# Checks and their sums placed otherwise in the score part, z on a third PSUM bank, one L tile given for a fifth row buffer

## The chip, the cores and the metric

The kernel runs on one core of a Trainium2 chip. Its engines are TensorE (PE, matrix products), VectorE (DVE), ScalarE (ACT), GpSimd (POOL) and SyncE (SP, which mostly issues transfers). Each takes its own list of instructions strictly in order, and they wait for one another by semaphores. What is measured is the device time of one execution in microseconds (us); smaller is better.

## The reference

2048 rows of 512 numbers are normalised, and three things are added up for each: the row itself, a Fourier mixing (FNet), and a layer of 4096 tiny experts, of which each of 32 heads picks two by a product of two key sets.

```python
x = A_x;  xn = layernorm(x)                       # (1, 2048, 512)
# FNet: real part of the transform along both axes
a = einsum("bsd,ed->bse", xn, dft_hid_re);  b = einsum("bsd,ed->bse", xn, dft_hid_im)
fnet = einsum("ts,bse->bte", dft_seq_re, a) - einsum("ts,bse->bte", dft_seq_im, b)
# product-key experts: 32 heads, two scores of 64 keys each, K = 2
q = einsum("nd,dhc->nhc", xn, w_q);  q1, q2 = q[..., :128], q[..., 128:]
s1 = einsum("nhd,ed->nhe", q1, k1);  s2 = einsum("nhd,ed->nhe", q2, k2)
i1, i2 = top2(s1), top2(s2);  t1, t2 = the scores there
cand = t1[..., :, None] + t2[..., None, :];  top_s, top_e = top2 of the four
g = softmax(top_s)                                # weights of 2 experts per head
act = gelu(einsum("nd,nhkd->nhk", xn, u[top_e]))  # u, v: (4096, 512)
out = x + fnet + einsum("nhk,nhk,nhkd->nd", g, act, v[top_e])
```

## The kernel before

**Layout.** The 2048 rows are 16 row blocks of 128. Three parts follow one another. The Fourier part takes the first 75 us and is not touched. The **score part** (about 75 to 470 us) runs 8 rounds `j`, four heads each, over 16 row blocks `i`; step `16*j + i` is the number `n` by which the tables of the code place work. The **expert part** (about 470 to 1137 us) computes the layer for 14 of the 16 blocks with dense products over all 4096 experts, and for the last two blocks row by row from gathered expert rows (`NS = 2`).

**One step of the score part.** `scores` runs 12 matmuls into a PSUM tile `s` (L796; four banks in turn), ACT copies it to the tile `ss` (L801), and DVE takes the maxima and their places from `ss` (L804, L808). A bank of `s` is free for PE again only when ACT has copied it. Beside this the engines prepare later work, each piece hung behind a given step: pieces of u and v split into two halves (`fill_uv`: ACT L606 and L607, then POOL L608), the next query weights (ACT L161, POOL L169), `m_stage` (PE L147, ACT L222), and `routing` of the round before, on POOL and DVE (L645 to L689).

**Checks.** The kernel tests symmetries of the Fourier matrices, since it uses only part of them. 32 checks are "early": `check_load` loads a tile `cx` (pool of 3 buffers) three steps ahead; at step `n` its differences are taken on POOL (`cx[k][0]`: L752, L758, and for some L760, L773); later ACT adds up their absolute values (`cx[k][1]`: L778, 896 numbers a partition). `hold` hangs a piece behind a given matmul in the order of DVE, ACT and POOL. The table `at_k` gives the steps.

**One block b of the expert part.** `u_part` computes z for 8 groups of columns `cg`, 48 matmuls of 128 columns each (L956), into a PSUM bank; ACT turns each bank into `act` (L959). `g_mm` builds for each of 4 groups of 32 tokens one-hot tiles on DVE: two tiles `L` (L980), taken in turn from the list `LS`, and one `R` (L988, L991) from `RS`; 32 matmuls turn them into g (L993). `w_part` multiplies act by g on DVE (`w`, L1004), ACT casts it (L1011), DVE takes the rest (L1014). `v_part` is 96 matmuls into one bank `pv` (L1023), and `finish` adds it to y on DVE (L1038). PE's order in one block is z groups 0 to 2, g group 0, z 3 to 6, g 1, z 7, 36 matmuls of v of the block before, g 2, 48 of v, g 3, the last 12 of v, and the next block.

**PSUM banks there.** `pb` has two banks, `pc` two, `pg` four (two tiles g of two banks). z takes the banks of `pb` in turn. One bank of `pc` holds `px`, the row block in use by the gathered rows, for as long as its 64 rows last; the other is `pv`.

**Gathered rows.** 128 rows (2 blocks of 64 pairs of head and pick) pass, spread evenly over the blocks, through `fetch` (POOL L1049: an indirect transfer of 128 rows of u and v together into a tile `ga` of 4 KB a partition, `BUFS` tiles in turn), `dot` (DVE L1065), `gain` (ACT L1075 to L1078, POOL L1083 adds to the output), after which the next fetch is issued. DVE also runs the later checks and ACT their sums.

Of the kernel before, what the change touches and what calls it, by code (L numbers as in the profile page):

```python
# [10 lines left out]
F16 = mybir.dt.float16  # L11
# [8 lines left out]
P = 128  # L20
# [16 lines left out]
def tile_fnet_peer(ctx, tc, x, ca, cb, c5, wt, wf, wr, wq, kt, ut, vn, uv, out):  # L37
# [518 lines left out]
    def part_b(safe, stS, stP, stE, xt, u_sb, cmp_p):  # L556
# [55 lines left out]
        z = sp.tile([P, NT, 3, 2, 2, H], F16, name="z")  # L612
# [90 lines left out]
        def follow(i, after):  # L703
            tc.add_manual_dep(i, after.ins.name, mybir.DependencyInfo(
                mybir.DependencyClass.NoSync, mybir.DependencyReason.DATA), reason="pace")

        def hold(f, after, engines=(mybir.EngineType.DVE, mybir.EngineType.Activation, mybir.EngineType.Pool)):
            made = nc.cur_bb.bb.instructions
            first = len(made)
            f()  # L710
            for i in made[first:]:
                if i.engine in engines:
                    follow(i, after)
                if i.engine == mybir.EngineType.Activation and after.ins.name in GL:
                    follow(i, GL[after.ins.name])
# [109 lines left out]
        else:  # L825
# [7 lines left out]
            for j in range(1, NCH):  # L833
                for t in range(4):
                    todo[1 + t if j == 1 else (j - 1) * NT + 2 * t - 5].append(
                        lambda at, j=j, t=t: m_prep(j, t, wqp, sw))
# [10 lines left out]
        checks = {}  # L847
        cx = {}

        def check_load(k):  # L850
            cx[k] = compare(EARLY[k], k)

        at_k = [10, *(16 + i for i in (0, 4, 6, 7, 10)), *(16 * j + i for j in range(2, 7) for i in (0, 4, 6, 7)), 112, 125]
        assert len(at_k) == len(EARLY)
        for k, n in enumerate(at_k):
            checks.setdefault(n - 3, []).append(lambda mm, k=k: check_load(k))
            checks.setdefault(n, []).append(lambda mm, k=k: hold(cx[k][0], mm))
            checks.setdefault(n + 1, []).append(lambda mm, k=k: hold(cx[k][1], mm))
        XB = {}
        m_stage(1, wq_tile, 0)  # L860
        pend = None
        for j in range(NCH):
# [8 lines left out]
            for i in range(NT):  # L871
                spare, mm = scores(j, i, vals, idx)
# [37 lines left out]

        ap0 = stE.enter_context(tc.tile_pool(name="ap0", bufs=1, side="left"))
        lr = stE.enter_context(tc.tile_pool(name="lr", bufs=1, side="left"))
        LS = [lr.tile([P, 16, P], F16, name=f"L{k}") for k in range(3)]
        RS = [lr.tile([P, 32, NC], F16, name=f"R{k}") for k in range(2)]
        ap = [ap0, stE.enter_context(tc.tile_pool(name="ap1", bufs=1, side="left"))]

        def blk_tiles(b):
            if b == 1:
                xb = bp.tile([P, 2, 2, KD, P], F16, tag="ga", name="xb_1", bufs=BUFS)[:, 0]
            elif b:  # L920
                xb = xbp.tile([P, 2, KD, P], F16, tag="xb", name=f"xb_{b}", bufs=1)
            else:
                xb = XB[0]
            act = ap[b % 2].tile([P, NC, P], F32, tag="act", name=f"act{b}")
            return xb, act
# [2 lines left out]
        alloc_v(V2, 16)  # L928
        TG = 32
        WB = 4  # L930
        BUFS = 4
        BT = [blk_tiles(b) for b in range(2)]
        NB = NT if safe else NT - NS
        ACT = {}
# [11 lines left out]

        def u_part(b, cg):
            act, xb = ACT[b]
            p = (pc if b == 0 and cg % 4 > 1 else pb)(f"z{b}_{cg}")
            for cc in range(4):  # L950
                c = cg * 4 + cc
                ug = u_sb[c // 2]
                n = 0
                for kd in range(KD):
                    for l, r in ((0, 0), (0, 1), (1, 0)):
                        mm = nc.tensor.matmul(p[:, cc * P:(cc + 1) * P], ug[:, l, c % 2, kd, :],  # L956
                                              xb[:, r, kd, :], start=(n == 0), stop=(n == 3 * KD - 1))
                        n += 1
            GL[mm.ins.name] = nc.scalar.activation(act[:, cg * 4:cg * 4 + 4, :].rearrange("p c n -> p (c n)"), p,  # L959
                                                   AF.Gelu_apprx_tanh, scale=zsc)  # L960
            return mm
# [9 lines left out]
        def g_mm(b, tg, after=None):  # L971
# [5 lines left out]
            for hf in range(2):  # L977
                LS.append(LS.pop(0))
                L = LS[-1]
                nc.vector.tensor_tensor(  # L980
# [64 lines left out]
        def fetch():  # L1045
            if rows:
                n, s = rows.pop(0)
                t = T[n, s] = bp.tile([P, 2 * D], F32, tag="ga", name=f"ga{n}_{s}", bufs=BUFS)
                nc.gpsimd.indirect_dma_start(  # L1049
                    out=t, out_offset=None, in_=uv,  # L1050
                    in_offset=bass.IndirectOffsetOnAxis(ap=eix[:, n].rearrange("p k h -> p (k h)")[:, s:s + 1], axis=0))

        def dot(n, s):
            if s == 0:
# [6 lines left out]
                if n == 0:  # L1061
                    for _ in range(BUFS):
                        fetch()
# [157 lines left out]
        if not safe:  # L1221
            nc.vector.memset(chk[:, 68:70], 0.0)
            for k in range(0, len(EARLY), 16):
                n = min(16, len(EARLY) - k)
# [4 lines left out]
        for g in range(V2, 16 if not safe else V2):  # L1229
            i = nc.sync.dma_start(v_sb[g].rearrange("p l c d -> p (l c d)"), v_d[g - V2])  # L1230
# [7 lines left out]
        for cg in range(8):  # L1238
            u_part(0, cg)
            if cg in (4, 6):  # L1240
                g_mm(0, (cg - 4) // 2)
# [9 lines left out]
        for n in range(0 if safe else NS):  # L1251
            b = NB + n
# [5 lines left out]
        for b in range(NB):  # L1258
# [5 lines left out]
            for cg in range(8):  # L1264
# [3 lines left out]
                mm = v_part(b, pv, cg)  # L1268
# [32 lines left out]
            for cg in range(8 if b + 2 < NB else 0):  # L1301
                mm = u_part(b + 2, cg)
# [38 lines left out]
    with tc.If(rv > 0):  # L1341
        with tc.tile_pool(name="gen", bufs=1) as gp, \
# [20 lines left out]
            for q in range(4):  # L1363
                ya = gp.tile([P, 4, D], F32, tag="ya", name=f"gya{q}")
                for ri in range(2):
# [25 lines left out]
                    for a in range(4):  # L1391
                        py = pb(f"gy{q}{ri}{a}")
                        n = 0
# [9 lines left out]
                        b = 4 * q + a  # L1403
# [56 lines left out]
```

## Time and profile before

| | us |
|---|---|
| runs | 1145.79, 1149.62, 1151.56 (median 1149.62) |
| profiled execution, device time | 1146.11 |
| its span in the profile | 1144.3 |
| PE busy | 1079.9 (94%) |
| DVE busy | 981.6 (86%) |
| ACT busy | 716.1 (63%) |
| POOL busy | 624.5 (55%) |

The span is the time in which the engines' instructions lie; 1.8 us of the device time are around it. A row of the timeline gives the start, the duration, the engine, the line of the code, the operation and its tiles, and in brackets the idle time before it with the engine, tile and line that ended it. A row of the table of waits gives who waited for whom, the total in us, how many times and the longest. The profiled execution is 3.5 us below the median of the runs.

### The profile page before, as it was taken

The page shows a single profiled execution, that of the slowest core. Times are in us where ns is not written, and L with a number is a line of the kernel's source. Part 1 is how long each engine was busy: PE and PEld are TensorE (multiplying, and loading weights), DVE is VectorE, ACT ScalarE, POOL GpSimd, SP SyncE. Part 2 cuts the span into 40 slices and gives each one's busy share as a digit, 9 for nine tenths or more (in the row PEclk, how much of TensorE's full clock was granted, in tenths as well). Part 3 has the DMA queues.
Part 4 walks back from the last instruction along what each step waited for, and adds up shares of the span by engine and source line. Part 5 has one row for each costly group of instructions (what it writes and reads, how often), then busy time and mean ns, then how long its engine had stood idle before and what let it go on. Part 6 is the DMA issues. An engine that isn't in the chain of part 4 may idle for free. (4 is left out here: it accounts for less than half of the span.)

```text
span 1144.3 us, 28472 instructions
## 1 busy us (share of the span) xinstructions
PE 1079.9 (94%) x11070; PEld 699.4 (61%) x11070; DVE 981.6 (86%) x2786; ACT 716.1 (63%) x1324; POOL 624.5 (55%) x552
## 2 busy tenths in 40 slices
PE   5899998999999989999999899999979999999897
PEld 4354554454444544896776867868656686875853
DVE  6878797978888889978997989999989899996981
ACT  2566656768596667542766667667656766775650
POOL 0011657586776945210668486675556667666650
PEclk9799999999999999999999999999999999999999
DMA  8247163535444341263667477675765677666532
GB/s 318 80 180 244 50 219 101 187 126 168 162 152 144 114 139 63 67 209 95 191 216 238 149 224 243 214 222 186 215 211 154 213 225 235 228 210 191 161 84 49
DMA packets 84434, 196.73 MB, mean 172 GB/s; under 512 B 10295, under 2 KB 27070, under 8 KB 84289
## 3 DMA queue, kind: packets, MB, share of 16 engines
q1 hardware_dynamic: 63394, 123.49, 31.9%
q0 software_dynamic: 20736, 71.31, 21.3%
q8 instruction: 88, 1.44, 0.5%
q14 instruction: 58, 0.47, 0.1%
q10 hardware_dynamic: 158, 0.01, 0.0%
HBM read 177.68 MB, written 17.10 MB: 170 GB/s over the span
## 5 line engine op out<-in xcount | busy, mean ns | idle before, releaser
L796 PE MATMUL s<-m,xq 128*128 128x512 f16 x1536 | 343.8, 382 | 10.5 <-ACT ss L801 10.4
L956 PE MATMUL z<-xb,u 128*128 128x128 f16 x5376 | 310.6, 220 | 13.3 <-ACT act L959 13.1
L956 PEld LDWEIGHTS <-u 128*128 128x128 f16 x5376 | 303.9, 98 | 18.1 <-issue 14.7
L1023 PE MATMUL v<-v,act 128*128 128x512 f16 x1344 | 303.3, 383 | 1.5 <-DVE act L1014 1.5
L1083 POOL TENSOR_TENSOR ov<-ov,ga 128x512 f32<-128x512 f32 x128 | 190.6, 1489 | 189.0 <-ACT ga L1078 151.7
L796 PEld LDWEIGHTS <-xq 128*128 128x128 f16 x1536 | 149.1, 98 | 185.8 <-issue 17.7
L1023 PEld LDWEIGHTS <-act 128*128 128x128 f16 x1344 | 129.4, 99 | 151.6 <-issue 6.3
L1049 POOL DMA_INDIRECT ga<-in_uv_dram,eix x128 | 171.4, 1339 | 48.1 <-POOL ov L1083 35.3
L804 DVE MAX8 vals<-ss 128x8 f32<-128x64 f32 x1024 | 152.7, 216 | 26.3 <-ACT ss L801 26.3
L980 DVE TENSOR_TENSOR L<-io_lam,cmp 128x2048 f16<-128x2048 f16 x112 | 155.7, 1414 | 15.5 <-PE g L993 8.1
L778 ACT ACTIVATE cx<-cx 128x896 f32<-128x896 f32 x64 | 60.7, 948 | 104.1 <-POOL cx L758 48.8
L959 ACT ACTIVATE act<-z,scl 128x512 f32<-128x512 f32 x112 | 75.3, 676 | 75.3 <-PE z L956 69.9
L1065 DVE SCALAR_TENSOR_TENSOR ga<-ga,px 128x512 f32<-128x512 f32 x128 | 86.1, 677 | 32.9 <-DMA ga<-in_uv_dram,eix 31.7
L1011 ACT ACTIVATE act<-w 128x1024 f16<-128x1024 f32 x56 | 75.5, 1349 | 52.4 <-DVE w L1004 48.8
L808 DVE FIND_INDEX8 idx<-vals,ss 128x8 uint16<-128x256 f32 x256 | 107.1, 418 | 0.0
L1078 ACT ACTIVATE ga<-ga,za 128x512 f32<-128x512 f32 x128 | 92.1, 722 | 9.8 <-ACT za L1076 0.4
L801 ACT ACTIVATE ss<-s,wsc 128x512 f32<-128x512 f32 x112 | 73.9, 679 | 29.9 <-PE s L796 22.9
L1014 DVE TENSOR_TENSOR act<-w,act 128x1024 f16<-128x1024 f32 x56 | 83.4, 1491 | 3.6 <-ACT act L1011 3.6
L1004 DVE SCALAR_TENSOR_TENSOR w<-act,scl,g 128x1024 f32<-128x1024 f32 x56 | 70.8, 1269 | 1.2 <-PE g L993 0.8
L169 POOL TENSOR_TENSOR wq<-wq,wh 128x1024 f16<-128x1024 f32 x26 | 55.4, 2131 | 25.5 <-DMA wq<-in_wq_dram 16.8
L993 PE MATMUL g<-R,L 128*128 128x32 f16 x1792 | 53.7, 177 | 11.0 <-DVE w L1004 10.5
L993 PEld LDWEIGHTS <-L 128*128 128x128 f16 x1792 | 51.9, 96 | 18.3 <-issue 11.8
(274 smaller groups left out, 1303.6 us busy)
## 6 DMA issues: line engine op xcount, KB each, us to landing
cx<-in_cb_dram SPq DMA_DIRECT2D x64, 448.0 KB, 6.1
wq<-in_wq_dram SPq DMA_DIRECT2D x32, 512.0 KB, 5.1
fit<-in_wq_dram SPq DMA_DIRECT2D x28, 512.0 KB, 4.9
uv<-in_ut_dram SPq DMA_DIRECT2D x16, 512.0 KB, 3.6
uv<-in_vn_dram SPq DMA_DIRECT2D x16, 512.0 KB, 3.5
xq<-in_x_dram SPq DMA_DIRECT2D x8, 512.0 KB, 8.3
xt_d<-xq SPq DMA_DIRECT2D x16, 256.0 KB, 3.6
cx<-in_ca_dram SPq DMA_DIRECT2D x64, 64.0 KB, 3.8
```

Source lines behind the costliest of these rows:

```text
L796: mm = nc.tensor.matmul(ps, xt[i][:, l, kd, :], m[:, r, kd, :], start=(n == 0), stop=(n == 3 * KD - 1))
L804: nc.vector.max(vals[:, i, w, :, h], s[:, g, :])
L808: nc.vector.max_index(idx[:, i, w].rearrange("p k h -> p (k h)"), vals[:, i, w, 0:2].rearrange("p k h -> p (k h)"), s[:, w * HC:g + 1, :]. ...
L956: mm = nc.tensor.matmul(p[:, cc * P:(cc + 1) * P], ug[:, l, c % 2, kd, :], xb[:, r, kd, :], start=(n == 0), stop=(n == 3 * KD - 1))
L980: nc.vector.tensor_tensor(L.rearrange("p t (l two) -> p t l two", two=2), io_lam.rearrange("p (l two) -> p l two", two=2).unsqueeze(1).to_ ...
L993: i = nc.tensor.matmul(p[:, hf, t * NC:(t + 1) * NC], L[:, t, :], R[:, hf * 16 + t, :], start=True, stop=True)
L1014: nc.vector.tensor_tensor(w16[..., 1], w, w16[..., 0], op=ALU.subtract)
L1023: mm = nc.tensor.matmul(pv, w16[:, c, :, l], vg[:, r, c % 2, :], start=(c == 0 and k == 0), stop=(c == NC - 1 and k == 2))
L1049: nc.gpsimd.indirect_dma_start(out=t, out_offset=None, in_=uv, in_offset=bass.IndirectOffsetOnAxis(ap=eix[:, n].rearrange("p k h -> p (k h ...
L1065: nc.vector.scalar_tensor_tensor(t, t, 1.0, T["x"], op0=ALU.mult, op1=ALU.mult, accum_out=T["z", n][:, s:s + 1])
L1078: nc.scalar.activation(t, t, AF.Copy, scale=z)
L1083: T["a"] = nc.gpsimd.tensor_tensor(o, o, t, op=ALU.add)
```

## The change

Three things, with no instruction added or removed.

1. The table `at_k` is rewritten: in rounds 1 to 6 the checks lie at steps 0, 4, 7 and 9 of the 16 (before 0, 4, 6 and 7), so that no two follow within one step; one is taken from the start of round 2 and some single ones move. The sums lie two steps behind the differences, before one.
2. `LS` has two tiles instead of three, `ga` five buffers instead of four (the tile given up is as large as the one added).
3. From block 1 on, z groups 2 and 5 use the free bank of `pc` (the one of `pv`) and the other six the two banks of `pb`. Block 0 keeps its banks.

```diff
@@ -850,12 +850,12 @@
         def check_load(k):
             cx[k] = compare(EARLY[k], k)
 
-        at_k = [10, *(16 + i for i in (0, 4, 6, 7, 10)), *(16 * j + i for j in range(2, 7) for i in (0, 4, 6, 7)), 112, 125]
+        at_k = [7, 10, *(16 * j + i for j in range(1, 7) for i in (0, 4, 7, 9) if (j, i) != (2, 0)), 112, 122, 125]
         assert len(at_k) == len(EARLY)
         for k, n in enumerate(at_k):
             checks.setdefault(n - 3, []).append(lambda mm, k=k: check_load(k))
             checks.setdefault(n, []).append(lambda mm, k=k: hold(cx[k][0], mm))
-            checks.setdefault(n + 1, []).append(lambda mm, k=k: hold(cx[k][1], mm))
+            checks.setdefault(n + 2, []).append(lambda mm, k=k: hold(cx[k][1], mm))
         XB = {}
         m_stage(1, wq_tile, 0)
         pend = None
@@ -910,7 +910,7 @@
 
         ap0 = stE.enter_context(tc.tile_pool(name="ap0", bufs=1, side="left"))
         lr = stE.enter_context(tc.tile_pool(name="lr", bufs=1, side="left"))
-        LS = [lr.tile([P, 16, P], F16, name=f"L{k}") for k in range(3)]
+        LS = [lr.tile([P, 16, P], F16, name=f"L{k}") for k in range(2)]
         RS = [lr.tile([P, 32, NC], F16, name=f"R{k}") for k in range(2)]
         ap = [ap0, stE.enter_context(tc.tile_pool(name="ap1", bufs=1, side="left"))]
 
@@ -928,7 +928,7 @@
         alloc_v(V2, 16)
         TG = 32
         WB = 4
-        BUFS = 4
+        BUFS = 5
         BT = [blk_tiles(b) for b in range(2)]
         NB = NT if safe else NT - NS
         ACT = {}
@@ -946,7 +946,7 @@
 
         def u_part(b, cg):
             act, xb = ACT[b]
-            p = (pc if b == 0 and cg % 4 > 1 else pb)(f"z{b}_{cg}")
+            p = (pc if cg in ((2, 3, 6, 7) if b == 0 else (2, 5)) else pb)(f"z{b}_{cg}")
             for cc in range(4):
                 c = cg * 4 + cc
                 ug = u_sb[c // 2]
```

**ACT in round 3, steps 5 to 11** (`ss3_5` is the copy of step 5 of round 3, `cx20` the sum of a check, `u10` a piece of u, `m4` the products for the next round). Before:

```order
L801 ACTIVATE ss3_5_2941<-s3_5_2928,wsc_93 128x512
L606 ACTIVATE u10_131<-uv0_10_2805,usc_102 128x1024
L607 ACTIVATE uv0_10_2805<-uv0_10_2805,usc_102 128x1024
L801 ACTIVATE ss3_6_2994<-s3_6_2981,wsc_93 128x512
L778 ACTIVATE cx20_2832,early_91<-cx20_2832 128x896
L801 ACTIVATE ss3_7_3022<-s3_7_3009,wsc_93 128x512
L222 ACTIVATE m4_3090<-m4_0_2835,wsc_93 128x512
L222 ACTIVATE m4_3090<-m4_1_2842,wsc_93 128x512
L222 ACTIVATE m4_3090<-m4_2_2849,wsc_93 128x512
L222 ACTIVATE m4_3090<-m4_3_2856,wsc_93 128x512
L778 ACTIVATE cx21_2893,early_91<-cx21_2893 128x896
L801 ACTIVATE ss3_8_3077<-s3_8_3064,wsc_93 128x512
```

Now:

```order
L801 ACTIVATE ss3_5_2932<-s3_5_2919,wsc_93 128x512
L606 ACTIVATE u10_131<-uv0_10_2799,usc_102 128x1024
L607 ACTIVATE uv0_10_2799<-uv0_10_2799,usc_102 128x1024
L778 ACTIVATE cx18_2734,early_91<-cx18_2734 128x896
L801 ACTIVATE ss3_6_2984<-s3_6_2971,wsc_93 128x512
L801 ACTIVATE ss3_7_3013<-s3_7_3000,wsc_93 128x512
L222 ACTIVATE m4_3078<-m4_0_2826,wsc_93 128x512
L222 ACTIVATE m4_3078<-m4_1_2833,wsc_93 128x512
L222 ACTIVATE m4_3078<-m4_2_2840,wsc_93 128x512
L222 ACTIVATE m4_3078<-m4_3_2847,wsc_93 128x512
L801 ACTIVATE ss3_8_3066<-s3_8_3053,wsc_93 128x512
L778 ACTIVATE cx19_2884,early_91<-cx19_2884 128x896
```

Before, two sums stand between the copies of steps 6 and 8, each one step behind its differences. Now one stands between the copies of steps 5 and 8, the next behind that of step 8, and each is two steps behind its differences.

**POOL at the start of round 2** (`c…`, `i2s…`, `di…` belong to `routing`, `wq3_2` is a piece of query weights, `cx14` a check). Before:

```order
L647 TENSOR_TENSOR c101_0_2107<-vals1_1337 128x64
L752 TENSOR_TENSOR cx14_1931<-cx14_1931 128x2x256
L752 TENSOR_TENSOR cx14_1931<-cx14_1931 128x256
L650 TENSOR_TENSOR c001_0_2105<-c011_0_2106,c001_0_2105 128x64
L667 TENSOR_TENSOR if1_0_2147<-if1_0_2147,hoff_94 128x256
L758 TENSOR_TENSOR cx14_1931<-cx14_1931 128x128
L672 TENSOR_TENSOR di1_0_2152<-if1_0_2147 128x128
L674 TENSOR_TENSOR c011_0_2106<-pm1_0_2108,di1_0_2152 128x64
L676 TENSOR_TENSOR i2s1_0_2109<-pm1_0_2108,di1_0_2152 128x64
L675 TENSOR_TENSOR c011_0_2106<-c011_0_2106,if1_0_2147 128x64
L169 TENSOR_TENSOR wq3_2_1797<-wq3_2_1797,wh3_2_2024 128x1024
L677 TENSOR_TENSOR i2s1_0_2109<-if1_0_2147,i2s1_0_2109 128x64
```

Now:

```order
L647 TENSOR_TENSOR c101_0_2100<-vals1_1343 128x64
L667 TENSOR_TENSOR if1_0_2140<-if1_0_2140,hoff_94 128x256
L650 TENSOR_TENSOR c001_0_2098<-c011_0_2099,c001_0_2098 128x64
L672 TENSOR_TENSOR di1_0_2145<-if1_0_2140 128x128
L674 TENSOR_TENSOR c011_0_2099<-pm1_0_2101,di1_0_2145 128x64
L676 TENSOR_TENSOR i2s1_0_2102<-pm1_0_2101,di1_0_2145 128x64
L675 TENSOR_TENSOR c011_0_2099<-c011_0_2099,if1_0_2140 128x64
L677 TENSOR_TENSOR i2s1_0_2102<-if1_0_2140,i2s1_0_2102 128x64
L169 TENSOR_TENSOR wq3_2_1800<-wq3_2_1800,wh3_2_2021 128x1024
```

The check is gone from this place, and the last step of the routing chain, L677, stands ahead of the weights.

**DVE between blocks 5 and 6 of the expert part** (`y4` is L1038 of block 4, `cmp6` the indices of block 6, from which its L and R tiles are made). Before:

```order
L988 TENSOR_TENSOR R0_5795<-io_c_73,cmp6_10170 128x1024
L1014 TENSOR_TENSOR act5_9376<-w5_1_10163,act5_9376 128x32x32
L991 TENSOR_TENSOR R0_5795<-R0_5795,cmp6_10170 128x1024
L980 TENSOR_TENSOR L1_5793<-io_lam_72,cmp6_10170 128x2048
L980 TENSOR_TENSOR L2_5794<-io_lam_72,cmp6_10170 128x2048
L988 TENSOR_TENSOR R1_5796<-io_c_73,cmp6_10170 128x1024
L752 TENSOR_TENSOR cx29_10202<-cx29_10202 128x2x256
L752 TENSOR_TENSOR cx29_10202<-cx29_10202 128x256
L1065 SCALAR_TENSOR_TENSOR ga0_43_10149,za0_7125<-ga0_43_10149,px0_7124 128x512
L758 TENSOR_TENSOR cx29_10202<-cx29_10202 128x128
L1038 SCALAR_TENSOR_TENSOR y4_10176<-v4_10030,scl_101,y4_10176 128x512
L1004 SCALAR_TENSOR_TENSOR w5_2_10337<-act5_9376,scl_101,g5_2_10089 128x1024
```

Now:

```order
L1014 TENSOR_TENSOR act5_9377<-w5_1_10164,act5_9377 128x32x32
L980 TENSOR_TENSOR L0_5792<-io_lam_72,cmp6_10171 128x2048
L980 TENSOR_TENSOR L1_5793<-io_lam_72,cmp6_10171 128x2048
L988 TENSOR_TENSOR R1_5795<-io_c_73,cmp6_10171 128x1024
L752 TENSOR_TENSOR cx29_10203<-cx29_10203 128x2x256
L752 TENSOR_TENSOR cx29_10203<-cx29_10203 128x256
L1065 SCALAR_TENSOR_TENSOR ga0_43_10076,za0_7124<-ga0_43_10076,px0_7123 128x512
L758 TENSOR_TENSOR cx29_10203<-cx29_10203 128x128
L1038 SCALAR_TENSOR_TENSOR y4_10177<-v4_10031,scl_101,y4_10177 128x512
L1004 SCALAR_TENSOR_TENSOR w5_2_10338<-act5_9377,scl_101,g5_2_10090 128x1024
L1065 SCALAR_TENSOR_TENSOR ga0_44_10150,za0_7124<-ga0_44_10150,px0_7123 128x512
```

`y4` stands between the same neighbours, the dot of row 43 and `w5_2`. Of `cmp6` three L tiles stood before it and now two, since the third has no tile to go to until the first group's matmuls are done; R0 is made earlier. On PE the order of matmuls in a block is the same in both, except that in block 1 a few matmuls of v of block 0 stand earlier among those of g. What differs is a wait: the first matmul of z group 2 of blocks 2 to 13 waited for ACT's copy of an earlier group (L959), and now waits for DVE's L1038 of the block two before, which is the last reader of `pv` in that bank.

## The prediction

> **What bounds the kernel now.** I read the page's busy shares, then the table of PE's waits from 60 us on, then the windows of the two parts. The first two lines are from the page (PE's share, and its granted clock in 40 slices of 28.6 us); the next five are PE's waits; the last two are windows with span, then busy time of PE, PEld, DVE, ACT, POOL, clock and DMA.
>
> ```profile
> PE 1079.9 (94%) x11070; PEld 699.4 (61%) x11070; DVE 981.6 (86%) x2786; ACT 716.1 (63%) x1324; POOL 624.5 (55%) x552
> PEclk9799999999999999999999999999999999999999
> ...
> PE z L956 <- ACT act L959: 13.1, 11, 2.5
> PE g L993 <- DVE w L1004: 10.5, 5, 4.4
> PE s L796 <- ACT ss L801: 10.4, 7, 2.3
> PE m L147 <- DVE u L457: 3.9, 1, 3.9
> PE v L1023 <- DVE act L1014: 1.5, 1, 1.5
> ...
> 75.00:470.00 395.00, 379.63 (x2431) 190.26 (x2430) 338.05 (x1742) 272.32 (x411) 240.30 (x261) 0.99 0.43 143
> 470.00:1137.00 667.00, 641.23 (x8451) 476.30 (x8449) 584.96 (x880) 405.79 (x842) 376.88 (x275) 0.99 0.62 189
> ```
>
> PE is the bound in both parts: it idles 15.4 us of the score part and 25.8 us of the expert part, and no matmul is removed. So the change can win those 41 us at most, and what a late start costs in clock. The five waits are 39.4 us of them. Each part of the change is aimed by its place at one: the checks at s <- ss, the third bank at z <- act, the fifth row buffer at DVE's lateness (g <- w, v <- act).
>
> **The clock.** After some gaps the same matmuls run at half pace for about 3.4 us.
>
> ```profile
> 1046.21 0.95 PE L993 MATMUL g<-R,L 128*128 128x32 f16 x32 [2.21 <-DVE w L1004]
> 1047.01 7.03 PE L1023 MATMUL v<-v,act 128*128 128x512 f16 x24
> 1054.04 5.34 PE L1023 MATMUL v<-v,act 128*128 128x512 f16 x24
> ...
> 649.11 2.84 PE L956 MATMUL z<-xb,u 128*128 128x128 f16 x48 [2.42 <-ACT act L959]
> 651.78 0.95 PE L993 MATMUL g<-R,L 128*128 128x32 f16 x32
> 360.62 5.73 PE L796 MATMUL s<-m,xq 128*128 128x512 f16 x18 [2.29 <-ACT ss L801]
> 197.04 0.22 PE L147 MATMUL m<-sums,wh 128*128 128x64 f16 x2 [3.88 <-DVE u L457]
> 197.21 4.44 PE L796 MATMUL s<-m,xq 128*128 128x512 f16 x12
> ```
>
> 24 matmuls of v take 7.03 us behind the gap at 1046 and 5.34 at full pace: a spell costs 1.7 us. The gap of 2.42 at 649 had none (48 matmuls in 2.67 us to the next row), those of 2.29 and 3.88 had one (18 matmuls at 5.34/24 would be 4.0 us, not 5.73). I find six spells, behind gaps of 1.9 to 4.4 us. The Trainium skill ("TensorE: Matmul & The Clock Gate", section on HAM oscillation) says the rule is "no PE-idle gaps >~3.4µs". By it only the two longest gaps would cost a spell, and my sum below would hold two of them instead of four, 3.4 us less gain; the trace has them behind shorter gaps too, so I go by the rows.
>
> **The score part: checks.** The table of ACT's waits first, then POOL, ACT and PE around 310 us.
>
> ```profile
> ACT cx L778 <- POOL cx L758: 48.8, 14, 8.6
> ...
> 307.12 2.13 POOL L608 TENSOR_TENSOR u<-uv,u 128x1024 f16<-128x1024 f32 x1 [2.72 <-ACT uv L607]
> ...
> 310.80 0.95 ACT L778 ACTIVATE cx<-cx 128x896 f32<-128x896 f32 x1 [3.18 <-POOL cx L773]
> ...
> 311.75 0.67 ACT L801 ACTIVATE ss<-s,wsc 128x512 f32<-128x512 f32 x1
> ...
> 312.46 2.75 PE L796 MATMUL s<-m,xq 128*128 128x512 f16 x12 [2.05 <-ACT ss L801]
> ```
>
> ACT stands 3.18 us before the sum of a check, whose differences wait on POOL behind a piece of u (2.13 us) that itself waited for ACT; the copies of s stand behind that sum in ACT's list, and with four banks full PE stops. A step is 3.09 us (395/128). With the sum one step later, each of these waits of ACT loses about 3.1 us: of 14, mean 3.5, some 0.4 is left on average, the longest 5.5. Checks no longer follow in neighbouring steps, so POOL never has two of them with a piece of u between. The banks cover four steps, so I leave 1.0 of the 10.4 us: **-9.4**. The bounds are 0 (the longest waits fall where the banks are full) and -10.4. The spell at 361 goes with its gap: **-1.7**. The cost is the same work elsewhere: sums are 0.95 us of ACT each, 272 of 395 us busy, and differences lie on POOL, 240 of 395; both have room. The check moved to step 7 puts its differences on POOL ahead of an early reduction (L121) that leads to the first pieces of u and v at step 29; 20 steps lie between, so 0.
>
> **Start of round 2.** PE waited 3.88 us for DVE's L457, which stood behind routing (L681), which waited for POOL:
>
> ```profile
> 188.99 2.13 POOL L169 TENSOR_TENSOR wq<-wq,wh 128x1024 f16<-128x1024 f32 x1
> 191.08 0.32 POOL L677 TENSOR_TENSOR i2s<-if,i2s 128x64 f32<-128x64 f32 x1
> ```
>
> L677 now stands ahead of L169 (2.13 us), and the check's differences are gone from before it. That takes at least 2.1 off; I take 3.88 to 1.5: **-2.4** (bounds -2.1 and -3.9), short enough for no spell: **-1.7**. L169 comes 0.3 us later; its reader has a round's time. Score part: **-15.2** (bounds -3.8, with the checks worth nothing, and -17.7).
>
> **The expert part: third bank.** All eleven z gaps are PE waiting for ACT's copy of the group two before; the longest is 2.5 us. With banks for groups 0, 1, 3, 4, 6, 7 in turn and 2 and 5 apart, a group waits for a copy three groups back, 2.67 us more time, and the pair 7 to 1 has v between: **-13.1**, and the spell behind the 2.50 gap at 1075 **-1.7**. But group 2 now waits for L1038. Before, nobody on PE did: in the table of that line the only one who waited is POOL at the end. First the line's own group and that row, then starts of v's successor on PE and of L1038.
>
> ```profile
> L1038 DVE SCALAR_TENSOR_TENSOR y<-v,scl,y x14: 732/738/752, 536.4 to 1137.8; 128x512 f32<-128x512 f32 x14
> ...
>   POOL fr L1178: 6.0, 1
> ...
> 628.14 4.07 PE L956 MATMUL z<-xb,u 128*128 128x128 f16 x70
> 639.10 0.73 DVE L1038 SCALAR_TENSOR_TENSOR y<-v,scl,y 128x512 f32<-128x512 f32 x1
> ...
> 967.09 3.12 PE L956 MATMUL z<-xb,u 128*128 128x128 f16 x53
> 975.28 0.75 DVE L1038 SCALAR_TENSOR_TENSOR y<-v,scl,y 128x512 f32<-128x512 f32 x1
> ```
>
> Group 2 is wanted two groups (5.34 us) after v ends; L1038 takes 0.74. At 639.10, 10.96 us after 628.14, PE would wait 6.36; at 975.28, 3.59. Over the eleven blocks concerned, at DVE's old times: 22.0 us (nine above zero). Three of them (6.36, 3.56, 2.38) lie behind DVE's longest stalls:
>
> ```profile
> DVE ga L1065 <- DMA ga<-in_uv_dram,eix: 31.7, 18, 6.4
> DVE L L980 <- PE g L993: 8.1, 5, 5.7
> ...
> 625.59 0.69 DVE L1065 SCALAR_TENSOR_TENSOR ga<-ga,px 128x512 f32<-128x512 f32 x1 [6.39 <-DMA ga<-in_uv_dram,eix]
> ...
> 842.81 0.69 DVE L1065 SCALAR_TENSOR_TENSOR ga<-ga,px 128x512 f32<-128x512 f32 x1 [4.32 <-DMA ga<-in_uv_dram,eix]
> ...
> 856.66 1.01 PE L993 MATMUL g<-R,L 128*128 128x32 f16 x32 [4.37 <-DVE w L1004]
> ```
>
> **Fifth row buffer.** DVE stood 31.7 us for rows not yet landed, four stalls of 2.9 to 6.4 among them. Rows follow each other every 4.5 us (117 dots from 579 to 1108), so a fetch issued a row earlier saves about 4.5 us of each stall: of the 31.7 some 4 us stay. That removes the three waits above (12.3 us) and about 2.2 of the rest (small stalls of 0.85 us on average ahead of half of them): the L1038 term is **+7.5**, bounds 0 and 22.0. It also removes PE's gaps behind them (1.48 at 845, 3.4 of 4.37 at 857, 2.21 at 1046, 0.76 at 1072): **-7.8**, and one of their two spells **-1.7**; I keep the other, since DVE works close to PE's pace there.
>
> **Two L tiles.** A third tile let DVE build half a group ahead while PE used the others. Where DVE was ahead, it waits more (8.1 us rises), which costs nothing until it meets PE: the pair (two of 1.2 us) must fit between two groups of g, some 10 us apart. **+0.5**, bounds 0 and 2.4 (one pair late once).
>
> **What is late next.** DVE's own work:
>
> ```profile
> 535.57:581.10 45.53, 45.53 (x613) 34.21 (x612) 42.91 (x71) 30.69 (x65) 26.56 (x19) 1.00 0.63 196
> ...
> 771.01:818.26 47.25, 45.69 (x612) 34.23 (x611) 46.36 (x69) 32.56 (x71) 26.84 (x21) 1.00 0.66 204
> 818.26:872.68 54.42, 47.65 (x612) 34.63 (x611) 48.53 (x71) 32.95 (x70) 33.12 (x23) 0.97 0.62 190
> ```
>
> A block costs PE 45.53 us at best; in the two from 771 to 873 DVE has 94.9 us of work against 91.1, so 3.8 us of what is won there comes back, and with a small stall of a late check's load 1.4 more: **+5.2**, bounds 0 and 8. Expert part: -13.1 - 1.7 + 7.5 - 7.8 - 1.7 + 0.5 + 5.2 = **-11.1**.
>
> **Sum.** -15.2 - 11.1 = -26.3 on the profiled 1146.1 (span 1144.3 and 1.8 around it): 1119.8. That execution is 3.5 us under the median of the runs, 1149.6; against the median it is 1123.3.
>
> **Rivals.**
> - *Only the score part wins.* DVE is tied to PE by L1038 and two L tiles as much as rows release it: L1038's 22.0 instead of 7.5 and the g and v gaps stay (9.5 less gain), no give-back. For it: DVE has 585 of 667 us of work and a list written close to PE's. Against it: the stalls in front of the worst L1038 are just those a buffer shortens. -26.3 + 14.5 + 9.5 - 5.2 = -7.5: 1142.
> - *The checks stay late.* POOL's list is as long as before, and ACT's longest waits (8.6) exceed one step: s gaps and the spell at 361 stay, 11.1 less: 1134.
> - *All is won*: no L1038 wait and no give-back, 12.7 more: 1110.6. Against it: six L1038 waits without a long stall ahead.
> - *Slower.* L1038 lies behind a pair of L of the next block, and these now both wait for the last group of g of this one. If this puts L1038 later by d in every one of eleven blocks, PE waits 22 + 11 d. With the score part's -15.2, -13.1 and -1.7 against it, and the rows' gain used up, it decides (+5.7) from 22 + 11 d = 35.7, d = 1.25 us, one L tile. With a whole pair, 2.4 us, it is 22 + 26.4 - 30 = +18.4: 1168. Against it: one L tile fewer stands before L1038 than did, so it should rather come earlier.
>
> **How the numbers follow.** My forecast 0.55; only the score part 0.15; checks late 0.14; all won 0.08; slower 0.08. Predicted is the likeliest, 1123. The range runs from all won, 1110, to a little past the case of the score part alone, 1144. 0.5% of 1149.6 is 5.7 us, about what can be told from no change: faster is under 1143.9, slower over 1155.4. Faster holds the forecast, the checks' case, all won and half of the score part's alone, 0.85; slower 0.07, and 0.08 for between.
>
> **What would show it.** In the profile after: s <- ss at 1 us or so and the stage's end some 15 us earlier; z <- act gone and a row z <- DVE y L1038 in PE's waits of some 7 us (22 or more is the rival); ga <- DMA down to a few us; L <- PE g up; the last 8 slices of the clock without dips but one. The prediction is wrong if DVE's waits for rows stay (transfers, not buffers, limit them), if L1038 starts on average more than 6 us after v ends, or if ACT still stands for POOL with PE behind it.

## The result and the profile after

| us | before | changed |
|---|---|---|
| median of the runs | 1147.70 (1142.22 to 1151.56) | 1116.36 (1113.29 to 1122.64) |
| ratio, 95% interval | 1 | 0.9741 (0.9711 to 0.9771) |
| profiled span | 1144.3 | 1112.1 |
| to the first product of scores | 72.9 | 71.7 |
| score part, to the first z | 391.6 | 371.0 |
| expert part, to the end | 679.8 | 669.4 |

The changed kernel is 2.6% faster, 31 us by the medians; 1123 was predicted, 1110 to 1144 as the range. In the profile the score part gave 20.6 us (forecast 15.2) and the expert part 10.4 (forecast 11.1). One slip ahead of the prediction: there are 28 early checks and 40 late units, not 32 early ones; no term used that count.

The page of the changed kernel, PE's share and its granted clock in 40 slices of 27.8 us:

```profile
PE 1070.3 (96%) x11070; PEld 700.6 (63%) x11070; DVE 996.7 (90%) x2786; ACT 717.7 (65%) x1324; POOL 640.3 (58%) x552
PEclk9899999999999999999999999999998999999899
```

The table of PE's waits of the changed kernel from 60 us on, all of it:

```profile
PE z L956 <- DVE y L1038: 15.5, 6, 4.8
PE g L993 <- DVE w L1004: 1.9, 1, 1.9
PE g L993 <- DVE L L980: 0.2, 1, 0.2
```

The windows of the two parts, of the changed kernel and then of the kernel before between the same events (span, busy time of PE, PEld, DVE, ACT, POOL, clock, DMA):

```profile
71.70:442.70 371.00, 371.00 (x2344) 185.03 (x2342) 332.30 (x1710) 270.41 (x406) 241.32 (x261) 1.00 0.46 152
442.70:1112.10 669.40, 645.18 (x8552) 484.74 (x8549) 607.87 (x915) 410.72 (x849) 391.55 (x275) 0.99 0.62 189
```

```profile
72.90:464.50 391.60, 376.23 (x2344) 185.94 (x2343) 333.94 (x1709) 267.99 (x405) 240.30 (x261) 0.99 0.43 144
464.50:1144.30 679.80, 647.49 (x8551) 481.95 (x8548) 591.11 (x917) 411.24 (x850) 376.88 (x275) 0.99 0.61 186
```

The score part has no idle time of PE left, 371.00 of 371.00, and the clock stays full. In the expert part every old row of PE's waits went or shrank (z <- act 13.1, g <- w 10.5), and one new row came, larger than all that is left beside it: z waits for L1038. In the timeline of PE these are the places:

```profile
613.45 1.72 PE L956 MATMUL z<-xb,u 128*128 128x128 f16 x28 [2.71 <-DVE y L1038]
...
798.40 4.09 PE L956 MATMUL z<-xb,u 128*128 128x128 f16 x48 [2.67 <-DVE y L1038]
849.38 5.19 PE L956 MATMUL z<-xb,u 128*128 128x128 f16 x48 [3.96 <-DVE y L1038]
...
1040.08 5.28 PE L956 MATMUL z<-xb,u 128*128 128x128 f16 x48 [4.84 <-DVE y L1038]
```

The 48 matmuls behind a wait take 4.09 to 5.28 us at 798, 849 and 1040, where 2.7 is full pace: the slow spells now follow these waits. Before, the 13.1 us of z were eleven gaps of up to 2.5; now there are six of up to 4.84. The windows of three blocks (z to z) show which they are:

```profile
744.67:790.20 45.53, 45.53 (x612) 34.20 (x611) 45.39 (x66) 32.48 (x71) 26.66 (x21) 1.00 0.67 208
790.20:839.90 49.70, 47.02 (x612) 35.54 (x611) 49.23 (x71) 31.86 (x67) 33.21 (x23) 0.97 0.65 201
839.90:892.09 52.19, 48.21 (x613) 36.60 (x612) 48.03 (x62) 33.30 (x73) 32.30 (x24) 0.93 0.65 199
```

A block in which DVE works 45.39 us has PE at its 45.53 without a gap; where DVE works 48 to 49, PE waits. In the last of the three DVE itself stands for 4.2 us, 2.0 of them for PE's g: each engine waits for the other in turn. The row of DVE's stalls for gathered rows, 31.7 us before, is not in its table any more; L <- g went from 8.1 to 13.5 us.

### The profile page after: what moved, and what is told of

Same layout as the page of the kernel before. It is cut to its first block, busy times and chain, and to the rows that moved or that the text cites. A ratio compares the mean times of both kernels' runs of the same rounds, so it can differ in the third digit from the quotient of the medians.

```text
span 1112.1 us, 28462 instructions
## 1 busy us (share of the span) xinstructions
PE 1070.3 (96%) x11070; PEld 700.6 (63%) x11070; DVE 996.7 (90%) x2786; ACT 717.7 (65%) x1324; POOL 640.3 (58%) x552
## 3 DMA queue, kind: packets, MB, share of 16 engines
q8 instruction: 88, 1.44, 0.5%
## 5 line engine op out<-in xcount | busy, mean ns | idle before, releaser
L796 PE MATMUL s<-m,xq 128*128 128x512 f16 x1536 | 338.9, 379 | 0.0
L956 PE MATMUL z<-xb,u 128*128 128x128 f16 x5376 | 313.9, 221 | 15.5 <-DVE y L1038 15.5
L956 PEld LDWEIGHTS <-u 128*128 128x128 f16 x5376 | 307.6, 99 | 19.2 <-issue 16.4
L1083 POOL TENSOR_TENSOR ov<-ov,ga 128x512 f32<-128x512 f32 x128 | 203.5, 1590 | 167.2 <-ACT ga L1078 145.7
L1023 PE MATMUL v<-v,act 128*128 128x512 f16 x1344 | 298.6, 379 | 0.0
L980 DVE TENSOR_TENSOR L<-io_lam,cmp 128x2048 f16<-128x2048 f16 x112 | 157.8, 1441 | 13.5 <-PE g L993 13.5
L959 ACT ACTIVATE act<-z,scl 128x512 f32<-128x512 f32 x112 | 75.8, 679 | 97.2 <-PE z L956 96.3
L1014 DVE TENSOR_TENSOR act<-w,act 128x1024 f16<-128x1024 f32 x56 | 86.1, 1539 | 6.7 <-ACT act L1011 5.8
L1004 DVE SCALAR_TENSOR_TENSOR w<-act,scl,g 128x1024 f32<-128x1024 f32 x56 | 70.9, 1271 | 0.4 <-ACT act L959 0.2
```

The costliest lines, as they stand in the source:

```text
L796: mm = nc.tensor.matmul(ps, xt[i][:, l, kd, :], m[:, r, kd, :], start=(n == 0), stop=(n == 3 * KD - 1))
L980: nc.vector.tensor_tensor(L.rearrange("p t (l two) -> p t l two", two=2), io_lam.rearrange("p (l two) -> p l two", two=2).unsqueeze(1).to_ ...
L1014: nc.vector.tensor_tensor(w16[..., 1], w, w16[..., 0], op=ALU.subtract)
L1023: mm = nc.tensor.matmul(pv, w16[:, c, :, l], vg[:, r, c % 2, :], start=(c == 0 and k == 0), stop=(c == NC - 1 and k == 2))
L1083: T["a"] = nc.gpsimd.tensor_tensor(o, o, t, op=ALU.add)
```

## The experiments

All ratios are to the kernel before on the same chip; the changed kernel is 0.974 by its own comparison. Parts are read from one profile each, so differences of 2 to 3 us between them are not read.

| kernel | ratio, 95% interval | score part | expert part |
|---|---|---|---|
| before | 1 | 391.6 | 679.8 |
| the change, all parts | 0.9741 (0.9711 to 0.9771) | 371.0 | 669.4 |
| checks_only | 0.9805 (0.9778 to 0.9832) | 371.2 | 680.2 |
| rows_only | 0.9911 (0.9881 to 0.9942) | 391.0 | 669.8 |
| bank_only | 1.0117 (1.0093 to 1.0142) | 390.9 | 689.7 |
| no_bank | 0.9734 (0.9705 to 0.9762) | 371.4 | 672.5 |
| bank_3_6 | 0.9757 (0.9733 to 0.9780) | 372.0 | 672.5 |
| spread | 0.9713 (0.9689 to 0.9738) | 371.4 | 672.3 |
| spread_3_6 | 0.9704 (0.9682 to 0.9727) | 370.9 | 666.8 |
| spread_no_bank | 0.9727 (0.9708 to 0.9746) | 371.2 | 667.3 |
| heavy_out | 0.9658 (0.9614 to 0.9701) | 370.9 | 656.5 |
| pool_spread | 0.9840 (0.9796 to 0.9884) | 371.5 | 679.5 |
| sum2_L2 | 0.9879 (0.9823 to 0.9934) | 376.4 | 675.4 |
| more_early | 0.9687 (0.9663 to 0.9711) | 372.6 | 662.7 |

### The parts alone

**checks_only**: the kernel before with the new `at_k` and

```diff
-            checks.setdefault(n + 1, []).append(lambda mm, k=k: hold(cx[k][1], mm))
+            checks.setdefault(n + 2, []).append(lambda mm, k=k: hold(cx[k][1], mm))
```

> The kernel before with the new table and the sums two steps later, nothing else. Theory A (the three parts act in stages of their own and add up): the score part, 391.6 us before and 371.0 with all parts, takes 371 to 372, and the expert part stays at 679.8; about 20.6 us less than before, ratio 0.982. Rival B (what the score part won came in part from the other edits, by what lies at its end): no more than the 15.2 us that the prediction gave, ratio 0.987 or above.

Theory A, as expected: the windows are the changed kernel's score part and the old expert part.

```profile
72.60:443.80 371.20, 371.12 (x2345) 185.06 (x2343) 329.97 (x1710) 270.32 (x406) 241.40 (x261) 1.00 0.44 152
443.80:1124.00 680.20, 646.28 (x8551) 481.87 (x8548) 596.40 (x916) 410.73 (x849) 383.66 (x275) 0.99 0.59 186
```

**rows_only**: `range(3)` to `range(2)` for `LS`, `BUFS = 4` to `5`.

> The kernel before with five row buffers and two L tiles, nothing else. Theory A (DVE's stalls for rows are what makes g and v late): the row ga <- DMA falls from 31.7 us to under 4, PE's g <- w from 10.5 to about 2 and v <- act to 0, z <- act stays near 13, and one or two of the four slow spells of the expert part go: 10 to 13 us less, ratio 0.989 to 0.991. Rival B (two L tiles cost about what a row buffer wins): ga <- DMA falls, but L <- g grows past 20 us and g waits for L; ratio 0.997 to 1.003.

Theory A on the time, 10.0 us of the expert part. But the waits did not go where it said: g <- w stayed at 8.4 (2 was expected), and z <- act fell to 8.2 though no bank was added.

```profile
PE g L993 <- DVE w L1004: 8.4, 4, 2.6
PE z L956 <- ACT act L959: 8.2, 8, 2.5
```

**bank_only**: the changed line of `u_part`, nothing else.

> The kernel before with z on the third bank, nothing else: four row buffers, three L tiles. Theory A (the wait for L1038 is paid by DVE's lateness, which the rows' stalls add to): z <- act 13.1 goes, z <- y L1038 comes with about 22 us at DVE's old times, and slow spells follow its long waits (three to five of 1.7 us or twice that): the expert part is 5 to 15 us slower than before, ratio 1.004 to 1.013. Rival B (PE's wait at this place gives DVE the time that the old waits gave elsewhere, so it costs no more than in the changed kernel): z <- y L1038 about 15 us, ratio 0.997 to 1.002.

Theory A: 22.5 us of waits for L1038, the 22.0 worked out from DVE's old times, and the part is 9.9 us slower. Alone, the third bank is a loss.

```profile
PE z L956 <- DVE y L1038: 22.5, 8, 7.0
...
PE g L993 <- DVE w L1004: 8.5, 4, 2.8
```

**no_bank**: the changed kernel with the old line of `u_part`.

> The changed kernel without its third part: z in the two banks of pb again, new table and five row buffers kept. Theory A (DVE's load sets the expert part, and the bank only moves the place where PE waits for it): the two parts alone multiply to 0.9805 x 0.9911 = 0.972, and this kernel comes out there, the same as the changed kernel (0.974) or up to 3 us below it; z <- act returns with about 8 us and g <- w with about 8. Rival B (the bank wins what the prediction gave it, 13.1 and a spell for some 7.5 of waits for L1038): 5 to 8 us slower than the changed kernel, 0.979 to 0.981.

Theory A. The product of checks_only and rows_only is 0.9718, this kernel 0.9734, the whole change 0.9741: beside the fifth row buffer the bank brings nothing that can be told from zero. Where PE waits differs, the sum does not: 19.6 us here, 17.6 with the bank.

```profile
PE z L956 <- ACT act L959: 10.8, 10, 2.5
PE g L993 <- DVE w L1004: 8.3, 4, 2.4
```

**sum2_L2**: the kernel before, with `n + 1` to `n + 2` for the sums under the old table, and two L tiles with four row buffers.

> The kernel before with two single edits in parts that do not meet. In the score part the old table is kept and only the sums move from one step to two behind the differences. In the expert part there are two L tiles, with four row buffers as before. Score part (391.6 us before, 371.0 changed): theory A (the later sum is what frees ACT) s <- ss falls under 3 us, 376 to 382; rival B (neighbouring checks keep POOL late, whatever the step of the sum) s <- ss stays at 7 us or more, 386 or above. Expert part (679.8 before): theory A (a third tile is a cushion that PE never used) 678 to 682, L <- g up from 8 to 12 or more; rival B (two tiles cost what the row buffer had to win back) 685 or above.

Theory A in the score part. The later sum alone takes s <- ss to nothing and 15.2 us off the score part; of PE's waits there only the one at the start of round 2 is left (second fence, from the table of waits), and the rest, 5.4 us, is that gap and the slow spell behind it, which the new table takes. In the expert part two L tiles cost nothing that can be seen: it takes 675.4 us, 4.4 less than before and 2.6 below Theory A's range, and L <- g rose to 10.8 us, where 12 or more was expected. From one profile I don't read the difference.

```profile
73.50:449.90 376.40, 372.52 (x2345) 185.64 (x2344) 330.77 (x1707) 270.13 (x405) 240.40 (x261) 1.00 0.44 150
449.90:1125.30 675.40, 647.45 (x8551) 482.83 (x8547) 599.65 (x918) 411.40 (x849) 387.07 (x276) 0.99 0.61 188
```

```profile
PE m L147 <- DVE u L457: 3.9, 1, 3.9
```

### Is it the place of the wait, or DVE's work?

**bank_3_6**: `(2, 5)` to `(3, 6)`, so that PE asks for L1038 3.5 us later.

> The changed kernel with groups 3 and 6 of z on the bank of v, in place of 2 and 5. Group 3 starts one group of z and one of g (2.67 + 0.8 us) later than group 2. Theory A (L1038 is a little late, and PE asks for its bank too early): of the six waits of 0.6 to 4.8 us, 15.5 in all, only what is above 3.5 us is left, about 2 us, and the slow spells behind them go (8.5 us): 15 to 22 us less than the changed kernel, 0.955 to 0.961 of before. Rival B (DVE is the bound in these blocks): the same time is waited at g <- w, g <- L or v <- act of the same blocks, and it is within 5 us of the changed kernel, 0.970 to 0.978 of before.

Rival B by time. L1038 is nearly always in time now, and PE waits as long as before at other places. The row of v comes with the new place, though: v takes the bank that group 6 has just used and waits 5.5 us for ACT's copy of it.

```profile
PE g L993 <- DVE w L1004: 10.5, 5, 4.3
PE v L1023 <- ACT act L959: 5.5, 3, 2.6
PE z L956 <- DVE y L1038: 1.4, 1, 1.4
```

**spread**, **spread_3_6** and **spread_no_bank** run the late checks in another order, with the bank at groups 2 and 5, at 3 and 6, and not at all:

```diff
         todo_n = [n for n in range(68) if n not in EARLY]
+        heavy = [n for n in todo_n if n >= 64 or n // 8 % 4 == 0]
+        todo_n = [n for p in zip(heavy, [n for n in todo_n if n not in heavy]) for n in p]
```

> The changed kernel with the 40 late units of checks in another order: the 20 with the most work on DVE (those of the first column group, L739 to L743, and the four of L1121 to L1140) alternate with the 20 light ones; in the changed kernel they run in order of number, heavy ones together in the blocks from 559 to 654, from 790 to 892 and behind 1030. Same work. Theory A (DVE is the bound in just those blocks, 46.4, 49.2 and 48.0 us of work against PE's 45.5): its work evens out at 45.1 us a block, z <- y L1038 falls from 15.5 to under 5 us, of five slow units of 3.4 us in the expert part at most two stay: 12 to 20 us less, 0.957 to 0.964 of before. Rival B (L1038 stands too late in DVE's list whatever the load, behind a pair of L tiles that must wait for PE): waits of 1 to 4 us are found in other blocks, within 4 us of the changed kernel, 0.971 to 0.978.

> The same even order of the late checks, with z groups 3 and 6 on the bank of v. Theory A (DVE evened out): L1038 never late for group 3 and no more than 3 us at g <- w, but v <- act waits for the copy of group 6 as with the old order (5.5 us): 0.957 to 0.966. Rival B (order, not load): as bank_3_6, 0.973 to 0.978.

> The same even order of the late checks, with z in two banks. Theory A (once DVE has room, the bank is worth what it should be): z <- act stays with 8 to 13 us and one or two spells, g <- w goes: 8 to 13 us slower than the even order with the bank, 0.967 to 0.975. Rival B (the bank is worth nothing in any order): the same as the even order with the bank within 3 us.

The even order gave at most a few us: 0.9713, 0.9704 and 0.9727, none of them clear of the changed kernel's 0.9741. For `spread` Theory A missed by 0.7% at its nearest edge, and the time is Rival B's; `spread_3_6` lies between the two theories; `spread_no_bank` is within 3 us of `spread`, its Rival B: the bank is worth nothing in this order either. In `spread` the waits at 613, 798 and 849 went, and others of the same size came at 943 and 993:

```profile
943.41 4.47 PE L956 MATMUL z<-xb,u 128*128 128x128 f16 x48 [4.43 <-DVE y L1038]
993.26 1.95 PE L956 MATMUL z<-xb,u 128*128 128x128 f16 x32 [2.53 <-DVE y L1038]
1044.05 5.28 PE L956 MATMUL z<-xb,u 128*128 128x128 f16 x48 [4.87 <-DVE y L1038]
```

That is what Rival B said of the place. The next run tells its reason from Theory A's.

**heavy_out**: the differences of the 16 heavy checks of the first column group are left out, and ACT's sum of them is taken with factor 0 (that line is not shown).

```diff
                 def work():
-                    diff()
+                    if g:
+                        diff()
                     after(2, judge)
```

> The changed kernel, in which the 16 heavy late checks of the first column group load their tile but take no differences on DVE (L739 to L773, some 60 us of DVE in the expert part), and ACT's sum of them is taken with factor 0; everything else stays. Theory A (PE waits because DVE has as much work as PE there, and falls behind in its list): the five waits of 10.6 us for L1038 from 565 to 898 go with the three slow units of 3.4 us behind them, the one at 1040 (4.8 us, four other units of checks) stays: 13 to 17 us less than the changed kernel, 0.959 to 0.963 of before. Rival B (place in the list: L1038 behind a pair of L tiles that waits for PE): at least half of the 10.6 us stays, within 7 us of the changed kernel, 0.968 or above.

By time it lies between the two theories: 0.9658, 9.5 us under the changed kernel by the ratios and 12.5 by the profiles. By place it is Theory A: from 560 to 900 us the 10.6 us of waits for L1038 are 0.5 (two rows, of 0.33 and 0.19), beside one of 1.30 for w. DVE's list is otherwise the old one: of its 478 instructions for L, R, w, act, y and the dots, 18 stand elsewhere, by up to three places. The wait near 1026 (1040 in the changed kernel), where the four other units lie, stays with 2.90 us.

```profile
885.92 2.84 PE L957 MATMUL z<-xb,u 128*128 128x128 f16 x48 [0.19 <-DVE y L1039]
1025.79 4.47 PE L957 MATMUL z<-xb,u 128*128 128x128 f16 x48 [2.90 <-DVE y L1039]
1054.17 1.02 PE L994 MATMUL g<-R,L 128*128 128x32 f16 x32 [3.73 <-DVE w L1005]
```

(The lines stand one further down in this kernel.) So the waits go when DVE has less to do: its busy time in the part fell from 607.9 to 553.5 us. That spreading did not help fits this: with 45.1 us a block (mean of eleven in the changed kernel) against PE's 45.5 no block has room for what another has too much.

One rival stays open. Ahead of the waits at 613 and 849 some 4 us of a check's differences stand between the pair of L tiles and L1038 in DVE's list, so heavy_out takes away the amount of work and what stands just ahead of L1038 at once. A kernel with L1038 ahead of these differences was not run. For the amount speaks bank_3_6, where PE asks for L1038 later and waits for w instead.

### Two tries at giving DVE less

**pool_spread**: the even order, and the light checks' differences on POOL.

```diff
-            v_eng = nc.vector if at is None else nc.gpsimd
+            v_eng = nc.gpsimd if at is not None or g else nc.vector
```

> The changed kernel with the late checks in even order, and the 20 light ones' differences (L752, L758) on POOL, as the early ones are: some 39 us less work for DVE in the expert part, some 48 us more for POOL at the 2.4 us that an early check takes it. Theory A (DVE's load is the bound, 45 us a block against 45.5): with 41.5 us a block the waits for L1038, w and L fall under 6 us in all, and the slow units to one or two: 12 to 18 us less than the changed kernel, 0.958 to 0.964 of before. Rival B (what DVE gains, the gathered rows lose, since POOL issues their transfers and adds them up): ga <- DMA comes back with 10 us or more, 0.970 to 0.980.

Slower than the changed kernel, as Rival B had it, but by more than its range (0.984 against at most 0.980) and by another way: rows were late by 4.9 us only. The old fault of the score part is back: in the expert part ACT's waits for POOL's L758 are 32.0 us in 12 (1.5 in the changed kernel), and DVE's for L699 15.4 (5.4 there). The longest of the six waits for L1038, in time order, from the timelines of POOL, ACT, DVE and PE:

```profile
740.82 2.10 POOL L752 TENSOR_TENSOR cx<-cx 128x512 f32<-128x512 f32 x2
743.00 0.46 POOL L758 TENSOR_TENSOR cx<-cx 128x128 f32<-128x128 f32 x1
743.49 0.95 ACT L778 ACTIVATE cx<-cx 128x896 f32<-128x896 f32 x1 [6.67 <-POOL cx L758]
746.95 0.79 ACT L699 ACTIVATE cmp<-zt 128x768 f16<-128x768 f16 x1
747.77 1.18 DVE L988 TENSOR_TENSOR R<-io_c,cmp 128x1024 f16<-128x1024 f16 x1 [4.58 <-ACT cmp L699]
...
760.86 4.36 PE L956 MATMUL z<-xb,u 128*128 128x128 f16 x46 [5.06 <-DVE y L1038]
```

ACT stands 6.67 us before the sum of a check that POOL has not finished, the indices for the next block (L699) wait behind it, DVE waits 4.58 us for them, and L1038, with a heavy check's differences also ahead of it, comes late: PE waits 5.06. What made the five other waits is not shown.

**more_early**: the even order, groups 3 and 6, and six light checks made early ones, a fifth in each round at step 13.

```diff
-    EARLY = [*range(8, 24), *range(40, 52)]
+    EARLY = [*range(8, 24), *range(40, 56), 24, 25]
...
-        at_k = [7, 10, *(16 * j + i for j in range(1, 7) for i in (0, 4, 7, 9) if (j, i) != (2, 0)), 112, 122, 125]
+        at_k = [7, 10, *(16 * j + i for j in range(1, 7) for i in (0, 4, 7, 9, 13) if (j, i) != (2, 0)), 112, 122, 125]
```

> An attempt at a faster kernel: the changed kernel with z groups 3 and 6 on the bank of v, the late checks evenly mixed, and six of the light late checks made early ones (a fifth in each of rounds 1 to 6, at step 13, on POOL). The score part has had no idle time of PE, and DVE loses some 12 us of the expert part's 495. Theory A (DVE's load in the expert part is what is left): the score part stays at 371 to 372, the waits of PE in the expert part fall below 10 us, 3 to 8 us less than the even order with the same banks: 0.964 to 0.968 of before. Rival B (the score part's POOL is full enough that a fifth check brings ACT's waits back): s <- ss returns with 3 us or more, and the time is that of the even order or above, 0.970 to 0.975.

Theory A in the score part, which stays almost free of waits; the expert part is the shortest of the kernels that compute everything, but PE still waits 13.7 us there, where less than 10 was expected. In time it gained 2 us on spread_3_6, less than the 3 to 8 expected, and its interval (0.9663 to 0.9711) only touches the changed kernel's. DVE's busy time in the expert part is 600.2 us, 7.7 less than in the changed kernel, where 12 less was expected. PE's waits, from 60 us on:

```profile
PE g L993 <- DVE w L1004: 6.9, 5, 2.2
PE z L956 <- ACT act L959: 5.8, 4, 2.0
PE g L993 <- DVE L L980: 1.0, 1, 1.0
PE m L147 <- POOL wq L169: 0.5, 1, 0.5
PE s L796 <- ACT ss L801: 0.2, 1, 0.2
```

## Why the prediction was right, and where not

**Time and sign: right.** 1116 against 1123, inside the range. The error of 7 us in the medians is made of the terms below; in the profile it is 5.9. Of that, 1.2 us lie ahead of the score part, which the change does not touch. That the expert part came within 0.7 us of its sum is luck: 7.3 us were booked for a bank that brought nothing measurable, and 5.2 of give-back and 1.0 too little for the row buffer set most of that off.

**Score part: the mechanism right, the size short by 5.4.** The gaps of s went whole (10.4, forecast 9.4), and so did the one at round 2 (3.88, forecast 2.4) and a wait for the weights of 1.0 that I gave no term. PE's busy time fell by 5.2 us, of which the two slow spells are 3.4. What I credited to sums and spaced checks together, sum2_L2 gives to the sums alone. The lower bound that I kept, that the longest waits of 8.6 us outlast one more step, did not come: ACT's waits for POOL's L758 fell from 48.8 us in 14 to 12.2 in 5, with the longest 4.2 (row below, of the changed kernel). I take it that a sum which no longer holds ACT no longer holds the pieces of u for which POOL then waited; no run takes that link apart. The average in the prediction, 3.5 less 3.1, would also have come out too low: a wait shorter than a step goes to nothing and not below it.

```profile
ACT cx L778 <- POOL cx L758: 12.2, 5, 4.2
```

**Third bank: the step that failed.** -13.1 for z and +7.5 for L1038, a gain of 5.6 and a spell. The first half was seen (z <- act gone). The second was 15.5, twice the term, and no_bank shows the net at nothing. Its working took the waits at DVE's old times less the stalls of rows; but DVE, freed of its stalls, was still late in the blocks with heavy checks. Over the eleven blocks L1038 started 5.7 us after the end of v (the start of PE's next z), against 6.6 before; more than 6 was named as a sign of being wrong. The give-back of +5.2, which I booked apart, is the same lateness seen at another row: 7.5 + 5.2 = 12.7 is near the 15.5 measured. That the two are one is argued from the places, and no run takes them apart.

**Row buffer: right in sum, not in place.** -7.8 and a spell were forecast, rows_only gave 10.0 for this and two L tiles. But there g <- w fell by 2.1 only and z <- act by 4.9, and the clock was at half pace for 13.7 us as before, so that the sum came out is in part luck. The stalls went whole (31.7 to 0; 4 was left in the forecast). Two L tiles: +0.5 forecast, nothing measurable found. What the prediction did not have: with the stalls gone, DVE's instructions in this part, the same as before, took longer in sum, 607.9 us in the changed kernel and 607.6 in rows_only against 591.1 before. Checks_only, which does not touch the part, reads 596.4, so some 5 us of this may be chance.

**Clock.** I let two of the four spells of the expert part go. By the granted clock in the trace it had 13.7 us at half pace before and has 17.1 now: 3.4 behind the wait at 798, and 6.8 each behind those of 3.96 and 4.84 us, twice the length of a spell.

**The rivals.** "Only the score part wins" had the price of L1038 right (22.0 against 22.5 in bank_only) where rows are not freed. "Slower" did not come, since L1038 was not later by a common amount in all blocks, but late only where DVE had much to do.

## What to carry to other kernels

A sum or any reader that stands in an engine's list for a slow producer holds everything behind it; moving that one reader a step later won 15 us here and cost nothing, and in pool_spread, where POOL became the producer and the reader was not moved, the same wait of ACT came back. When two engines have almost equal work, look at the work before the single wait of the one for the other: here a bank, another place of the wait or another order moved 15 to 20 us of waits from row to row, and of the edits tried only heavy_out, which took 54 us off DVE, brought them clearly down, to 8.6 us. Price a new dependency by the lateness of its producer in the blocks with the most work, and do not book "late there" and "work exceeds there" as two terms.

## What the runs showed of the hardware

The same DVE instruction does not always take the same time in the expert part. In the changed kernel, from 560 to 1040 us, the same instruction has these shortest, median and longest durations in ns:

```profile
L980 DVE TENSOR_TENSOR L<-io_lam,cmp x81: 1198/1212/2876, 559.9 to 1031.9; 128x2048 f16<-128x2048 f16 x81
L991 DVE TENSOR_TENSOR R<-R,cmp x40: 674/692/2475, 566.7 to 1027.2; 128x1024 f16<-128x1024 f16 x40
L1004 DVE SCALAR_TENSOR_TENSOR w<-act,scl,g x39: 1255/1271/1327, 567.3 to 1017.8; 128x1024 f32<-128x1024 f32 x39
...
L1083 POOL TENSOR_TENSOR ov<-ov,ga x110: 1267/1290/6042, 559.7 to 1037.5; 128x512 f32<-128x512 f32 x110
```

L980 and L991, which read two tiles of SBUF, stretch to more than twice their median, POOL's add to almost five times; L1004, one of whose tiles lies in PSUM, does not stretch. Between 560 and 900 us, of the L991 that stand alone in the timeline, 15 that no POOL add or issue of `add_x` overlaps take 0.69 us on average, and 10 that overlap one by over 0.5 us take 1.44 (eight of them more than 1 us; `add_x` is POOL's transfer that adds x to y, L1032). The Trainium skill ("Trainium Architecture — The Big Picture", section "What this means for kernel authors") says that DVE and GpSimd share a port pair under an exclusive lock; the rows agree for eight of the ten, but no run here takes POOL's adds away, so the cause is argued and not shown. Of L980 alone, 112 times a mean of 1441 against a median of 1212 is 26 us of DVE's time. It may be why pool_spread, with some 39 us of work (the estimate of its expectation) moved to POOL, lowered DVE's busy time by 18 us only (607.9 to 589.8).

The clock's slow spells were again no matter of the gap's length alone: none behind the wait of 2.71 us at 613, one behind 2.67 at 798.
